# First scores of the first batch read from the feature rows in halves of 64, with the regrouping kept for what follows

## The chip, the cores and the metric

The kernel runs on one core of a Trainium2 chip. The metric is the device time of one execution in microseconds (us); the figure compared is the median over several runs. One execution was also recorded by the hardware profiler. The engines are named as in the profile: PE (TensorE matmul) with PEld (its weight loads), DVE (VectorE), ACT (ScalarE), POOL (GpSimd) and SP (the queue that issues the transfers).

## The reference

Four batches, 8 heads, 768 steps, 48 features a head. First a linear attention whose state decays by a complex factor at each step, then a mixture of four attention experts over its output, of which each row takes two.

```python
def _attn_ref(q, k, v, a_re, a_im):          # B, H, S, D = 4, 8, 768, 48
    mag = np.sqrt(a_re * a_re + a_im * a_im)
    scale = np.minimum(mag, 0.999) / (mag + 1e-06)
    a_re_n, a_im_n = (a_re * scale, a_im * scale)
    for t in range(S):
        new_re = ar * S_re - ai * S_im       # ar, ai: step t's factor
        new_im = ar * S_im + ai * S_re
        S_re, S_im = (new_re + k[t] v[t]^T, new_im)
        y[:, :, t] = q[t] . S_re

def _moe_ref(x, w_gate, wq, wk, wv, wo):     # 4 experts of width 64, 2 for each row
    logits = x @ w_gate                      # top 2, softmax over them -> w
    for e in range(E):
        q, k, v = x @ wq[e], x @ wk[e], x @ wv[e]
        a = softmax(causal(scale * q @ k^T))
        ye = a @ v @ wo[e]
        out += (w of e where e is among the row's two) * ye
```

## The kernel before

All work is recorded as a list of operations and then issued in one written order: ORDER is a permutation of the list, HOME moves single operations to another engine, ROOMS says which buffer each tile gets, and FILL[i] puts so many matmuls without a use (512 columns of a constant, written to the bank that operation i is about to write) ahead of operation i. Each engine takes its instructions strictly in that order. So what an engine does next is fixed, and an instruction that waits holds up all that stand behind it on its engine. SP takes the transfers in that order too.

A batch has three thirds of 256 steps (k = 0, 1, 2), each of two chunks of 128 steps (c = 0 to 5). For a third, `logs`, `atan`, `angles`, `sincos` and `products` turn the decay (`ab`) and q, k (`qk`) into features: the running decay is folded into q and k as exponentials and as a cosine and a sine part. This is elementwise work of ACT, DVE and POOL on tiles of 128 partitions by 768 (three groups j of 128 feature rows by 256 steps); for the very first third the three groups are worked one by one, on 256 elements. The features end in `qk`, with the 384 (head, feature) pairs along j and the partitions. Attention wants each head's 96 rows (48 cosine, 48 sine) on 96 partitions, so `regroup` copies `qk` to `fm` by ten transfers a third.

`head(b, c)` then does two things for a chunk. It transposes k (`pk`, through `ident`, copied to `kts`), and it computes the scores of the chunk's 128 steps against themselves: `psc`, one matmul of 96 rows for each head, masked with `keep` into `pts` by DVE. `state` adds v against `kts` (`pu`) to the running state and scales it with the decay at the chunk's end, a column of `fm` (`tst`). `tail` sums `pts` against v and q against the state (`yu`) and splits the result into the two parts `x` of the experts' input; after each second chunk two transfers move the last heads' rows of `x`. From there `proj` (`pp`), `vproj` (`pv`), `maxpass` (`pm`) and the experts' attention (`score`, `av`, `norm`, `wo`) go on. While PE works on one third, the others make the features of the next ones.

At the start, PE's order is: 141 fills; `psc` and `pk` of chunk 0; one fill; `yu` of chunk 0; 14 fills; `pu` of chunk 0; `psc` of chunk 1; 7 fills; `pk` and `yu` of chunk 1; `psc` of chunk 2 (its first half); `pu` of chunk 1; and so on until the first `pp`.

Of the kernel before, what the change touches and what calls it, by code (L numbers as in the profile page):

```python
# [42 lines left out]
HOME = {26: 'gpsimd',  # L43
 32: 'gpsimd',
 40: 'vector',
 48: 'vector',
# [4 lines left out]
 134: 'vector',
 145: 'vector',
 150: 'gpsimd',
 169: 'gpsimd',
 183: 'gpsimd',
 199: 'vector',
 208: 'vector',
 213: 'vector',
 220: 'gpsimd',
 287: 'gpsimd',  # L60
 296: 'vector',
 303: 'vector',
 340: 'gpsimd',
 353: 'vector',
 424: 'gpsimd',
 437: 'gpsimd',
 459: 'gpsimd',
 473: 'gpsimd',
 497: 'gpsimd',
 503: 'gpsimd',  # L70
 505: 'gpsimd',
 513: 'gpsimd',
 549: 'gpsimd',
 551: 'gpsimd',
 563: 'gpsimd',
 571: 'gpsimd',
# [8 lines left out]
 619: 'gpsimd',
 630: 'gpsimd',
 631: 'gpsimd',
 632: 'gpsimd',
# [29 lines left out]
 1109: 'vector',
 1116: 'gpsimd',
 1135: 'vector',  # L120
 1167: 'gpsimd',
 1174: 'vector',
 1176: 'vector',
 1183: 'gpsimd',
 1187: 'vector',
 1192: 'vector',
 1199: 'vector',
 1201: 'vector',
 1227: 'vector',
 1240: 'vector',  # L130
 1313: 'gpsimd',
 1320: 'gpsimd',
 1328: 'gpsimd',
# [4 lines left out]
 1354: 'vector',
 1367: 'gpsimd',
 1369: 'gpsimd',  # L140
 1374: 'gpsimd',
 1381: 'vector',
# [12 lines left out]
 1493: 'gpsimd',
# [3 lines left out]
 1512: 'vector',  # L159
 1515: 'gpsimd',  # L160
 1520: 'gpsimd',
# [3 lines left out]
 1555: 'vector',
 1564: 'gpsimd',
 1579: 'vector',
 1580: 'vector',
 1583: 'vector',
 1608: 'vector',  # L170
 1619: 'vector',
 1622: 'vector',
 1624: 'vector',
 1640: 'vector',
 1643: 'vector',
 1647: 'vector',
 1708: 'vector',
 1709: 'vector',
 1712: 'vector',
 1761: 'gpsimd',  # L180
 1763: 'gpsimd',
 1776: 'gpsimd',
 1835: 'gpsimd',
 1856: 'vector',
 1857: 'gpsimd'}

FILL = {202: 141, 204: 14, 206: 1, 210: 7, 357: 3, 406: 2, 1873: 4}

ROOMS = {'ab': [0, 1, 0, 1, 0, 1, 0, 1, 0, 1, 0, 1],
 'carry': [0, 3, 2, 3, 2, 1, 1, 3, 1, 2],  # L190
 'fm': [0, 1, 0, 1, 0, 1, 0, 1, 0, 1, 0, 1],
# [30 lines left out]

ORDER = [13, 35, 20, 0, 34, 14, 19, 33, 15, 6, 17, 118, 1, 2, 4, 18, 3, 5, 8, 119, 9, 12, 21, 120, 22, 67, 36, 68, 185, 52, 69, 53, 70, 154, 37, 54, 71, 7,
# [68 lines left out]


class View:
# [85 lines left out]
def mid(x):  # L380
    return x.bitcast(F32)
# [548 lines left out]
```

## Time and profile before

| | |
|---|---|
| median of 3 runs | 414.89 us (413.98 to 415.06) |
| profiled execution | 413.87 us, of which the span of the trace is 412.2 us |
| busy in the span: PE, DVE, ACT, POOL | 398.0, 346.3, 280.3, 157.5 us |
| PE's first matmul that is no fill | at 38.77 us |
| PE's fills before it | 141, from 6.04 us on |
| chunk 2's first score matmul | at 57.28 us |
| first `pp` of batch 0 | at 64.44 us |

Times within the trace count from the span's start. A busy share counts fills as work, so PE's 398.0 us hold a first stretch in which it does nothing that the result needs. What ends first in each stage, and who is waited for there, is read from the stage's own rows.

### The profile page before, as it was taken

To read this page: it belongs to the slowest core of one execution; us is meant where nothing else is said; L and a number is where in the kernel's file an instruction comes from. 1 tells how busy PE (TensorE), PEld (TensorE's weight loads), DVE (VectorE), ACT (ScalarE), POOL (GpSimd) and SP (SyncE) were. 2 spreads that over 40 slices of the span, in tenths; PEclk is the share of its full clock that TensorE was granted. 3 is DMA by queue.
4 is the path that set the end of the run, shared out by engine and by line. 5 is a ranking of instruction groups with operands and counts; after the bars stand their busy time and mean duration, and the time that the engine had idled before them with its cause. 6 is when DMAs were issued, how large, how long until landed. Compare 5 with 4: busy or idle time off the path is not lost. (4 is left out here: it accounts for less than half of the span.)

```text
span 412.2 us, 9649 instructions
## 1 busy us (share of the span) xinstructions
PE 398.0 (97%) x3792; PEld 326.9 (79%) x3792; DVE 346.3 (84%) x738; ACT 280.3 (68%) x436; POOL 157.5 (38%) x146
## 2 busy tenths in 40 slices
PE   4999799999999999999999999999999999999996
PEld 1445579998888779989887789989779789887775
DVE  5997979999999999999999898798794556978751
ACT  6979788986898898879688999733533222124572
POOL 0002233559373444563263324640166634002440
PEclk9999989999999999999999999999999999999999
DMA  7767808875946506828424703628003510111002
GB/s 266 281 158 202 231 0 214 231 218 132 342 117 190 154 37 164 233 63 269 126 71 116 212 3 116 191 76 233 9 2 76 165 27 2 38 45 54 2 13 103
DMA packets 27261, 53.40 MB, mean 130 GB/s; under 512 B 3536, under 2 KB 7376, under 8 KB 27216
## 3 DMA queue, kind: packets, MB, share of 16 engines
q1 hardware_dynamic: 27216, 52.78, 44.2%
q8 instruction: 30, 0.49, 0.5%
q14 instruction: 15, 0.12, 0.1%
HBM read 26.74 MB, written 4.72 MB: 76 GB/s over the span
## 5 line engine op out<-in xcount | busy, mean ns | idle before, releaser
L871 POOL TENSOR_TENSOR qk<-qk,ab 128x768 f32<-128x768 f32 x20 | 40.0, 2011 | 64.2 <-DVE qk L871 49.1
L871 ACT ACTIVATE pe<-pss 128x1024 f32<-128x1024 f32 (+2 forms) x48 | 43.4, 915 | 26.0 <-PE pss L871 22.4
L871 POOL TENSOR_SCALAR_AFFINE_SELECT pe<-pe 128x256 f32<-128x256 f32 x48 | 25.3, 544 | 84.8 <-ACT pe L871 54.8
L871 PE MATMUL pp<-x,whi 128*128 128x256 f32 x288 | 55.6, 287 | 0.1
L871 PE MATMUL psc<-fm 96*128 96x128 f32 x384 | 52.1, 281 | 0.2
L871 PEld LDWEIGHTS psc<-fm 96*128 96x128 f32 x384 | 46.6, 192 | 3.2 <-issue 0.9
L871 ACT ACTIVATE ab<-ab 128x768 f32<-128x768 f32 (+1 forms) x61 | 45.8, 762 | 4.3 <-DVE ab L871 3.2
L871 PEld LDWEIGHTS pp<-x,whi 128*128 128x128 f32 x288 | 45.4, 189 | 1.5 <-issue 1.5
L871 ACT ACTIVATE qk<-qk 128x768 f32<-128x768 f32 (+3 forms) x64 | 43.1, 684 | 4.0 <-DVE qk L871 3.6
L871 PE MATMUL pss<-qka 64*128 64x256 f32 (+3 forms) x480 | 45.5, 301 | 0.1
L871 PE MATMUL po<-pe,v 128*64 128x256 f32 (+3 forms) x320 | 42.8, 395 | 0.8 <-POOL pe L871 0.8
L869 ACT ACT_TABLE_LOAD x33 | 42.3, 1283 | 1.3 <-PEq L919 0.8
L871 POOL TENSOR_TENSOR pe<-pe 128x512 f32<-128x512 f32 (+2 forms) x25 | 31.7, 1267 | 28.6 <-DVE pe L871 13.3
L860 PEld LDWEIGHTS <-keep 128*128 128x128 bf16 x172 | 17.2, 102 | 29.8 <-issue 6.8
L871 PEld LDWEIGHTS pss<-qka 64*128 64x128 f32 x480 | 35.7, 185 | 6.2 <-issue 2.4
L871 PE MATMUL pp<-x,wlo 128*128 128x256 f32 x144 | 40.3, 280 | 0.0
L860 PE MATMUL psc<-keep 128*128 128x512 bf16 x141 | 32.9, 398 | 6.0 <-DVE keep L871 6.0
L871 DVE TENSOR_TENSOR pts<-psc,keep 128x512 f32<-128x512 f32 x48 | 32.3, 682 | 5.3 <-PE yu L871 2.9
L871 POOL TENSOR_TENSOR qk<-qk 128x768 f32<-128x768 f32 x16 | 25.8, 1620 | 23.6 <-ACT qk L871 23.4
L871 DVE CUSTOM_DVE_ANT_0 junk<-pm,negm 128x128 bf16<-128x128 f32 (+3 forms) x64 | 31.1, 485 | 3.3 <-PE pm L871 2.1
L871 PEld LDWEIGHTS po<-pe,v 128*64 128x64 f32 x320 | 20.7, 136 | 14.9 <-issue 5.0
L871 PE MATMUL pv<-whi,x 128*128 128x260 f32 x144 | 31.1, 292 | 0.0
(121 smaller groups left out, 930.6 us busy)
## 6 DMA issues: line engine op xcount, KB each, us to landing
fm<-qk SPq DMA_DIRECT2D x72, 192.8 KB, 4.7
qk<-in_ak_dram SPq DMA_DIRECT2D x12, 768.0 KB, 5.7
ab<-in_ak_dram SPq DMA_DIRECT2D x22, 384.0 KB, 4.0
vt<-in_vk_dram SPq DMA_DIRECT2D x12, 512.0 KB, 5.9
out_dram<-ob SPq DMA_DIRECT2D x24, 192.0 KB, 1.9
fm<-qk SPq DMA_DIRECT2D x24, 128.5 KB, 4.1
x<-x SPq DMA_DIRECT2D x24, 96.0 KB, 3.0
fm<-qk SPq DMA_DIRECT2D x24, 64.2 KB, 4.2
```

What stands on the lines that cost most here:

```text
L860: nc.tensor.matmul(z, real(plan.busy), real(plan.busy)[:, None, :].to_broadcast([128, 4, 128]), start=True, stop=True)
L869: nc.scalar.preload_act_table_set(need)
L871: getattr(getattr(nc, engine), name)(*a, **k)
```

## The change

For the first third of the first batch, chunks 0 and 1 no longer read `fm`. The features' rows are laid out anew by the host: each group j of 128 rows now holds one head in rows 0 to 47 and another in rows 64 to 111, and the two halves' last 16 rows hold the sixth part of heads 6 and 7. So a half of 64 rows holds a head's 48 feature rows, once in slot 0 and once in slot 1 of `qk`, and the scores of six heads are matmuls of 48 rows from `qk` itself, two that add up for each head. Heads 6 and 7 are gathered by two transfers into a new tile `hx` (`spread`). The transposes of these two chunks take all 128 rows of `qk` at once (six a chunk in place of eight). For this third `regroup` moves only what is left to read: the second chunk's q and the two decay columns. For all thirds it is eight transfers in place of ten. K and Q change places in `qk`.

```diff
-    def regroup(b, k, js=(0, 1, 2)):
+    def regroup(b, k, js):
         if (b, k) not in fm:
             fm[b, k] = p.tile([96, H, KW], F32, "fm")
-        for h, d, j, r, n in pieces():
-            if j in js:
-                p.dma(fm[b, k][2 * d:2 * d + 2 * n, h], qk[k][r:r + n, j])
+        o = C2 + C if b == k == 0 else 0
+        for j in js:
+            for i in range(2):
+                x = qk[k][64 * i + D:64 * i + 64, :, :, o:] if j == 3 else qk[k][64 * i:64 * i + D, j, :, o:]
+                p.dma(fm[b, k][:, 2 * j + i, o:], x)
+
+    hx = p.tile([128, 2, 2 * C2], F32, "hx", "pe")
+    def spread():
+        for i in range(2):
+            p.dma(hx[64 * i:64 * i + D], qk[0][64 * i + D:64 * i + 64, :, :, :2 * C2])
...
     def head(b, c):
+        k, first = c // 2, b == 0 and c < 2
+        s = slice(c % 2 * C, c % 2 * C + C)
...
+            if first:
+                pj = pk.rearrange("p (j d) -> p j d", j=3)
+                for j in range(3):
+                    p.flip((pj[:, j], qk[k][:, j, g, s], ident))
...
+        if first:
+            z = p.bank("psc", 2).rearrange("p i (j t) -> p i j t", j=4)
+            for j in range(4):
+                t = hx if j == 3 else qk[0][:, j]
+                p.mm(*((z[:, i, j], t[64 * i:64 * i + D, x, s], t[64 * i:64 * i + D, x, C2 + c * C:C2 + c * C + C], x == 0, x == 1)
+                       for x in range(2) for i in range(2)))
...
-FILL = {202: 141, 204: 14, 206: 1, 210: 7, 357: 3, 406: 2, 1873: 4}
+FILL = {201: 39, 212: 9, 214: 21, 369: 1, 381: 3, 418: 1, 1864: 3}
...
-ORDER = [13, 35, 20, 0, 34, 14, 19, 33, 15, 6, 17, 118, 1, 2, 4, 18, 3, 5, 8, 119, 9, 12, 21, 120, 22, 67, 36, 68, 185, 52, 69, 53, 70, 154, 37, 54, 71, 7,
...
```

ORDER, HOME and ROOMS are new throughout, so the order shifts on every engine. Three places matter for what follows.

On PE at the start of the program, this stood before (each score and transpose reads `fm`; the rows of the 141 fills ahead are left out):

```order
L860 LDWEIGHTS keep
L860 MATMUL psc<-keep 128x512
L871 MATMUL psc<-fm 128x128 x8
L871 MATMUL pk<-ident,fm 128x96 x8
L860 LDWEIGHTS keep
L860 MATMUL yu<-keep 128x512
L871 MATMUL yu<-pts,vt 64x128 x8
```

and this stands there now, chunks 0 and 1 together, the 39 fills (written to the bank of `pk`) and the 21 fills (bank of `yu`) shown by one row each:

```order
L903 MATMUL psc<-qk 128x128 x16
L892 LDWEIGHTS keep
L892 MATMUL pk<-keep 128x512
...
L903 MATMUL pk<-ident,qk 128x128
L903 MATMUL psc<-hx 128x128 x4
L903 MATMUL pk<-ident,qk 128x128 x10
L903 MATMUL psc<-qk 128x128 x4
L903 MATMUL psc<-hx 128x128 x4
L903 MATMUL psc<-qk 128x128 x4
L892 LDWEIGHTS keep
L892 MATMUL yu<-keep 128x512
...
L903 MATMUL yu<-pts,vt 64x128 x8
```

Half of the two chunks' scores now come ahead of the fills; the other half, and all transposes, come behind a transpose that reads `ident`.

On DVE, `ident` was made among the first instructions; before, the products of third 1 (three on DVE) were followed at once by chunk 0's masking:

```order
L871 CAST pick<-ident 32x24
L871 TENSOR_TENSOR qk<-qk,ab 128x3x256 x3
L871 TENSOR_TENSOR pts<-psc,keep 128x512 x2
L871 COPY kts<-pk 128x384
L871 SCALAR_TENSOR_TENSOR qk<-qk 128x3x256
```

Now `ident` is made behind all four products of third 1, and eleven instructions on third 2, on the second batch and on the weights (`wlo`) come ahead of the masking:

```order
L903 TENSOR_TENSOR qk<-qk,ab 128x3x256 x4
L903 TENSOR_SCALAR ident<-iota 128x128
L903 SCALAR_TENSOR_TENSOR qk<-qk 128x3x256
L903 SCALAR_TENSOR_TENSOR ab<-col,carry,ab 128x256 x3
L903 SCALAR_TENSOR_TENSOR qk<-qk 128x3x256
L903 TENSOR_TENSOR wlo<-wst,whi 128x768
L903 SCALAR_TENSOR_TENSOR qk<-cmask,qk 128x256 x3
L903 TENSOR_TENSOR ab<-ab 128x768
L903 TENSOR_TENSOR wlo<-wst,whi 128x768
L903 TENSOR_TENSOR pts<-psc,keep 128x512 x2
L903 COPY kts<-pk 128x2x3x16
```

On SP, the second batch's q and k of third 0 (the tile of `qk` that chunks 0 and 1 now read on PE) are fetched ahead of the eighth transfer of third 1, and the transfers of `x` stand behind both:

```order
L903 DMA fm<-qk 96x1x514 x7
L903 DMA qk<-in_ak_dram 128x3x512
L903 DMA fm<-qk 96x1x514
L903 DMA qk<-in_ak_dram 128x3x512
L903 DMA x<-x 16x3x512 x2
```

Before, the same fetch stood ahead of third 1's transfers too, but what read its tile was the transfers of third 0 alone.

## Rows read from the trace of the kernel before

**Rows 1.** Busy time by stage: stretch, its length, each engine's busy (instructions), PE clock, DMA.
```profile
25.54:38.84 13.30, 13.30 (x64) 6.14 (x62) 11.91 (x19) 10.98 (x15) 0.72 (x1) 1.00 0.79 201
38.84:57.27 18.43, 16.15 (x135) 11.62 (x133) 14.65 (x20) 13.41 (x17) 5.75 (x3) 0.91 0.58 167
57.27:64.44 7.17, 6.71 (x78) 5.97 (x77) 7.04 (x11) 5.02 (x8) 3.89 (x2) 1.00 0.10 27
64.44:250.00 185.56, 183.79 (x1883) 159.50 (x1882) 177.47 (x363) 161.43 (x243) 89.08 (x71) 1.00 0.56 160
```

**Rows 2.** Timeline of PE to 65 us: start, length, line, tiles, count [idle before].
```profile
6.04 32.89 PE L860 MATMUL psc<-keep 128*128 128x512 bf16 x141 [6.04 <-DVE keep L871]
38.77 1.95 PE L871 MATMUL psc<-fm 96*128 96x128 f32 x16
40.55 0.82 PE L871 MATMUL pk<-ident,fm 96*128 96x96 f32 x8
41.52 1.09 PE L871 MATMUL yu<-pts,vt 128*64 128x128 f32 x16
51.44 2.96 PE L860 MATMUL pk<-keep 128*128 128x512 bf16 x7 [1.94 <-DVE tst L871]
56.30 1.04 PE L871 MATMUL yu<-fm,tst 96*48 96x128 f32 x16
57.28 1.16 PE L871 MATMUL psc<-fm 96*128 96x128 f32 x8
58.27 1.48 PE L871 MATMUL pu<-vt,kts 128*96 128x48 f32 x16
64.44 0.36 PE L871 MATMUL pp<-x,whi 128*128 128x256 f32 x1
```

**Rows 3.** Timeline of DVE, 22 to 62 us.
```profile
22.78 2.76 DVE L871 TENSOR_TENSOR qk<-qk,ab 128x256 f32<-128x256 f32 x8
...
27.73 1.27 DVE L871 TENSOR_TENSOR_SCAN qk<-cmask,qk 128x256 f32<-128x256 uint8 x2
...
30.43 0.95 DVE L871 TENSOR_TENSOR wlo<-wst,whi 128x768 fp32r<-128x768 f32 x1
31.29 0.55 DVE L871 TENSOR_SCALAR ab<-ab 128x768 int32<-128x768 int32 x1
...
50.84 0.54 DVE L871 TENSOR_TENSOR tst<-pu,fm 96x384 f32<-96x384 f32 x1
```

**Rows 4.** Timeline of PE, 68 to 72 us: 64-row matmuls between 96-row ones.
```profile
68.77 1.05 PE L871 MATMUL psc<-fm 96*128 96x128 f32 x8
69.77 0.73 PE L871 MATMUL pm<-qka 64*128 64x128 f32 x8
```

**Rows 5.** Busy time around PE's 1.94 us of idling (columns as in rows 1).
```profile
49.50:51.44 1.94, 0.00 (x2) 0.00 (x0) 1.94 (x3) 1.04 (x2) 1.94 (x2) 1.00 0.49 124
51.44:52.40 0.96, 0.96 (x3) 0.38 (x3) 0.96 (x2) 0.96 (x2) 0.96 (x1) 0.61 0.02 6
52.40:54.20 1.80, 1.80 (x6) 0.69 (x5) 0.78 (x2) 1.77 (x3) 0.20 (x1) 0.50 0.00 0
```

**Rows 6.** Groups by shape, ACT and DVE: count, busy us, mean ns.
```profile
L869 ACT ACT_TABLE_LOAD x33 | 42.3, 1283 | 1.3 <-PEq L919 0.8
L871 ACT ACTIVATE ab<-ab 128x768 f32<-128x768 f32 x50 | 41.8, 840 | 4.2 <-DVE ab L871 3.2 <-POOL ab L871 0.7
L871 ACT ACTIVATE x<-yu 128x512 fp32r<-128x512 f32 x19 | 11.3, 594 | 21.8 <-PE yu L871 21.7
L871 DVE TENSOR_TENSOR qk<-qk,ab 128x768 f32<-128x768 f32 x24 | 22.7, 958 | 1.2 <-ACT ab L871 0.9
```

**Rows 7.** Transfers by kind, from the page: count, KB each, median us to landing.
```profile
fm<-qk SPq DMA_DIRECT2D x72, 192.8 KB, 4.7
qk<-in_ak_dram SPq DMA_DIRECT2D x12, 768.0 KB, 5.7
```

**Rows 8.** Timeline of SP, 60 to 65 us.
```profile
60.69 1.27 SPq L871 DMA_DIRECT2D x<-x  x2
```

More of the change, by code (lines that the diff above doesn't have):

```diff
@@ L55 @@
  183: 'gpsimd',
+ 184: 'gpsimd',
  199: 'vector',
[L57 to L76, printed above, removed]
+ 205: 'vector',
+ 251: 'vector',
+ 285: 'gpsimd',
+ 292: 'vector',
+ 310: 'vector',
+ 320: 'vector',
+ 352: 'gpsimd',
@@ L77 @@
+ 380: 'vector',
+ 431: 'gpsimd',
+ 436: 'gpsimd',
+ 453: 'gpsimd',
+ 463: 'gpsimd',
+ 471: 'gpsimd',
+ 498: 'gpsimd',
+ 515: 'gpsimd',
+ 517: 'gpsimd',
+ 525: 'gpsimd',
+ 536: 'vector',
+ 561: 'gpsimd',
+ 576: 'gpsimd',
+ 577: 'gpsimd',
  583: 'gpsimd',
- 585: 'gpsimd',
- 596: 'gpsimd',
+ 594: 'gpsimd',
  597: 'gpsimd',
- 598: 'gpsimd',
- 599: 'gpsimd',
- 605: 'gpsimd',
+ 609: 'gpsimd',
+ 610: 'gpsimd',
+ 611: 'gpsimd',
  617: 'gpsimd',
[L85 to L88, printed above, removed]
@@ L118 @@
[L118 to L128, printed above, removed]
- 1227: 'vector',
[L130 to L133, printed above, removed]
+ 628: 'gpsimd',
+ 636: 'gpsimd',
+ 641: 'gpsimd',
+ 643: 'gpsimd',
+ 697: 'vector',
+ 743: 'gpsimd',
+ 747: 'vector',
+ 752: 'vector',
+ 759: 'vector',
+ 762: 'vector',
+ 794: 'gpsimd',
+ 822: 'vector',
+ 873: 'gpsimd',
@@ new lines @@
+ 878: 'gpsimd',
+ 913: 'gpsimd',
+ 940: 'gpsimd',
+ 945: 'gpsimd',
+ 949: 'gpsimd',
+ 951: 'gpsimd',
+ 957: 'gpsimd',
+ 959: 'gpsimd',
+ 967: 'gpsimd',
+ 969: 'vector',
+ 975: 'vector',
+ 978: 'vector',
+ 981: 'vector',
+ 991: 'gpsimd',
+ 1003: 'gpsimd',
+ 1010: 'gpsimd',
+ 1025: 'gpsimd',
+ 1037: 'gpsimd',
+ 1039: 'gpsimd',
+ 1052: 'gpsimd',
+ 1053: 'gpsimd',
+ 1059: 'gpsimd',
+ 1070: 'gpsimd',
+ 1073: 'gpsimd',
+ 1083: 'gpsimd',
+ 1084: 'gpsimd',
+ 1085: 'gpsimd',
+ 1086: 'gpsimd',
+ 1108: 'vector',
@@ L134 @@
+ 1120: 'gpsimd',
+ 1132: 'vector',
+ 1138: 'vector',
+ 1160: 'vector',
+ 1203: 'vector',
+ 1204: 'vector',
+ 1227: 'vector',
+ 1236: 'gpsimd',
+ 1249: 'vector',
+ 1254: 'vector',
+ 1263: 'vector',
+ 1333: 'gpsimd',
  1337: 'gpsimd',
  1339: 'gpsimd',
- 1345: 'gpsimd',
  1347: 'gpsimd',
[L138 to L142, printed above, removed]
  1382: 'gpsimd',
- 1387: 'gpsimd',
- 1399: 'gpsimd',
  1409: 'gpsimd',
  1411: 'vector',
- 1420: 'vector',
+ 1414: 'vector',
@@ L158 @@
  1501: 'gpsimd',
[L159 to L161 removed]
+ 1522: 'vector',
  1525: 'gpsimd',
+ 1526: 'gpsimd',
  1527: 'gpsimd',
  1528: 'gpsimd',
[L165 to L185, printed above, removed]
[L187 to L191 removed]
+ 1550: 'vector',
+ 1562: 'gpsimd',
+ 1566: 'vector',
+ 1571: 'vector',
+ 1577: 'vector',
+ 1578: 'vector',
+ 1581: 'vector',
+ 1602: 'vector',
+ 1604: 'vector',
+ 1642: 'vector',
+ 1645: 'vector',
+ 1646: 'vector',
+ 1671: 'vector',
+ 1702: 'vector',
+ 1789: 'gpsimd',
+ 1829: 'gpsimd',
+ 1851: 'gpsimd',
+ 1862: 'vector',
+ 1865: 'vector'}
+FILL = {201: 39, 212: 9, 214: 21, 369: 1, 381: 3, 418: 1, 1864: 3}
+ROOMS = {'ab': [1, 0, 1, 0, 1, 0, 1, 0, 1, 0, 1, 0],
+ 'carry': [3, 2, 0, 1, 3, 3, 3, 1, 1, 3],
+ 'fm': [1, 0, 1, 0, 1, 0, 1, 0, 1, 0, 1, 0],
  'gcf': [0, 0, 0, 0],
@@ L467, in views @@
         t = ab[b, k][:, :, g]
-        Q, K, X, Y = (qk[k][:, g, i, o:o + C2] for i in range(2) for o in (0, C2))
+        K, Q, Y, X = (qk[k][:, g, i, o:o + C2] for i in range(2) for o in (0, C2))
         return t[:, 0], t[:, 1], Q, K, X, Y
@@ L539, in head @@
         for g in range(2):
-            if c < NC - 1:
-                pk = p.bank("pk")[:, :384].rearrange("p (i d) -> p i d", i=4)
-                p.flip(*((pk[:, i], part(b, c, 4 * g + i, 1), ident[:96, :96]) for i in range(4)))
-                p.copy(kt[b, c][:, 4 * g:4 * g + 4], pk)
-        for g in range(2):
+            pk = p.bank("pk")[:, :384]
+            if first:
+                pj = pk.rearrange("p (j d) -> p j d", j=3)
+                for j in range(3):
+                    p.flip((pj[:, j], qk[k][:, j, g, s], ident))
+                p.copy(t[:, :6].rearrange("p h (d x) -> p x h d", x=2)[:, g], pk.rearrange("p (h d) -> p h d", h=6)[:, :, :D])
+                p.copy(t[:, 6:].rearrange("p i (r j x) -> p x i j r", j=3, x=2)[:, g],
+                       pk.rearrange("p (j i d) -> p i j d", j=3, i=2)[:, :, :, D:])
+            elif c < NC - 1:
+                pi = pk.rearrange("p (i d) -> p i d", i=4)
+                p.flip(*((pi[:, i], part(b, c, 4 * g + i, 1), ident[:96, :96]) for i in range(4)))
+                p.copy(t[:, 4 * g:4 * g + 4], pi)
@@ new lines, in head @@
+        if first:
[4 more added lines that the diff above has]
+                       for x in range(2) for i in range(2)))
+        for g in range(2):
+            pt[b, c, g] = p.tile([128, 4, C], F32, "pts")
+            if first:
+                o = pt[b, c, g].rearrange("p (j i) t -> p j i t", i=2)
+                p.mul(V, o, z[:, :, 2 * g:2 * g + 2].rearrange("p i j t -> p j i t"),
+                      keep[:, None, None, :].to_broadcast([128, 2, 2, C]))
+                continue
@@ L737, in norm @@
         dn = p.bank("dn")[:, :n]
-        left = [i for u in UNITS[g] for i in u if i not in SUMS[b][pr][g]]
-        p.mm(*((dn[64 * e:64 * e + 64, cols(g, i)[0] - t0:], onecols, pe[b, pr, g, i][:, e],
-                i == 0, i == left[-1]) for i in left for e in range(2)))
+        if (b, pr, g) in SPLIT_SUMS:
+            y = pe[b, pr, g, 0]
+            hi = p.tile([128, 2, 512], F32R, "hi", "pe")[:, :, :n]
+            lo = y.bitcast(F32R)
+            p.copy(hi, y)
+            p.tt(V, lo, y, mid(hi), OP.subtract)
+            p.mm(*((dn[64 * e:64 * e + 64], oner[:, :HD], x[:, e], x is hi, x is lo) for x in (hi, lo) for e in range(2)))
+        else:
+            left = [i for u in UNITS[g] for i in u if i not in SUMS[b][pr][g]]
+            p.mm(*((dn[64 * e:64 * e + 64, cols(g, i)[0] - t0:], onecols, pe[b, pr, g, i][:, e],
+                    i == 0, i == left[-1]) for i in left for e in range(2)))
         if (b, g) not in ot:
@@ L787, in record @@
                 load_v(b, c // 2)
-                for j in range(3):
+                if b == c == 0:
+                    spread()
+                for j in range(4):
                     regroup(b, c // 2, (j,))
```

105 lines of the change are left out of this document (39 added, 66 removed), and 166 rows, old and new, of tables (ORDER, ROOMS).

## The prediction

> **What bounds the kernel now.** I read the busy time by stage first [rows 1]. From 57.27 us on, PE is the engine that is never free: 6.71 of 7.17 us, then 183.79 of 185.56. A microsecond that PE gains ahead of 57 us is therefore a microsecond of the end, unless another engine can't follow; the one that might not is DVE, busy for 177.47 of those 185.56 us. Before 57 us it is the other way round: the timeline of PE [rows 2] shows 141 fills up to 38.77, 14 fills and a wait behind the first `yu`, 1.94 us without work up to 51.44 and seven more fills. In that stretch PE waits for features that DVE and ACT make: from 25.54 to 38.84 DVE is busy for 11.91 of 13.30 us and ACT for 10.98 [rows 1]. So the question is not how early PE can begin, but when it starts chunk 2, from where on it doesn't stop: at 57.28 now, with the 1.48 us of chunk 1's `pu` still to do [rows 2]. The place to compare is thus 57.28 + 1.48 = 58.76, since the new order has that `pu` behind it when chunk 2 starts.
>
> **What the change removes.** The wait for the regrouping of the first third. Its features are complete at 22.78 + 2.76 = 25.54 [rows 3], and PE's scores begin 13.2 us later. DVE's instructions up to that point are the same but for a handful of small ones in both directions, so I keep 25.5. Half of the scores of chunks 0 and 1 can then run at 22 to 27 us.
>
> **What it puts there instead.** The other half stands behind a transpose that reads `ident`, and DVE makes `ident` only after the products of third 1. From 25.5, DVE has ten instructions on 768 elements (0.86 each when they follow each other, from 30.43 to 31.29 [rows 3]), five scans (two in 1.27 with the pipeline's overlap, 0.60 each), one scalar instruction of 0.55 and `ident` of about 0.2: 8.6 + 3.0 + 0.55 + 0.2 = 12.4, so 37.9 without a wait. In the same stretch DVE now idles 13.30 - 11.91 = 1.4 us for ACT [rows 1], which bounds it above at 39.3. I take 38.6. So PE goes on at the same moment as before (38.77); what it won is that chunk 1 comes along.
>
> From there two branches run to the masking (`pts`). *DVE's own:* three instructions of 0.86 and six scans of 0.60, 6.2 us, to 44.8; then `ab`, `wlo` and two `pts` (0.86, 0.86, 1.3), to 47.8. *By way of PE:* eleven transposes of 128 columns (eight of 96 take 0.82 [rows 2], so 0.14 each, 1.5 us) and four groups of scores, each of eight passes over half the rows. Such passes have no row with these operands. The nearest is `pm`, eight passes over 64 rows and 128 columns in 0.73, against 1.05 for eight of 96 rows [rows 4]; at most they cost the latter, and if two halves ran fully side by side 0.5. I take 0.73: 2.9 us. That ends at 43.0. ACT may only then overwrite the slot of `qk` that the scores read; its two instructions (0.84 each [rows 6]) end at 44.7, just when DVE arrives. But PE has idled by then: at 32.89 / 141 = 0.23 us each [rows 2] the 39 fills take 9.1 us and end at about 36, 2.6 us early, or less early if they too begin slowly. What that does to the clock is shown by the stall of 1.94 us: the granted clock behind it is 0.61 and then 0.50, the lower of the two levels (1.2 GHz), from 51.44 to 54.2 at least [rows 5]. In 2.8 us at that level half the work is done, so PE's part ends 1.4 us later, ACT's at 46.1, and `pts` comes at 49.1. Ends 47.8 and 49.1; I take 48.5, since the idling may be shorter than the row's or longer.
>
> The Trainium skill (TensorE: Matmul & The Clock Gate, the section on HAM oscillation) says that waits between bursts of matmuls throw the array back to the half clock and that each burst then starts cold. The trace agrees at 51.44; by the rule alone the sum would take 49.1, by the fills that run straight into the scores at 38.77 it would take 47.8.
>
> **From the masking to chunk 2.** *DVE's own:* three instructions on 768 elements, one scalar one, two copies of `kts`, a tiny one, and three on 512 elements (0.65 each): 2.6 + 0.55 + 0.7 + 0.1 + 1.95 = 5.9, then `tst` 0.54. That gives 54.9. *By PE and ACT:* `yu` 1.09, ACT's `x` 0.59, a table load 1.28, two instructions of 0.84 and a small copy of `kts` 0.25, then the last of `pu` 0.5 and `tst` 0.54: 5.9, so 54.4. DVE decides. Each hand-over between engines costs something that such a sum hasn't: from 38.84 to 57.27 DVE now idles 3.8 us [rows 1]. I add 1.0 of it (bounds 0 and 2.5). Then `yu` against the state, 1.04 [rows 2], and chunk 2 starts at 57.0. With all lower ends it is 54.5, with all upper ones 60.0.
>
> **The rest.** The gain is 58.76 - 57.0 = 1.8 us, with bounds +4.3 and -1.2. PE's other work is the same instruction for instruction; of the fills behind 57 us there are five before and after, and at the end three in place of four, worth 0.2. Two transfers a third less, and the moves of single operations between DVE, ACT and POOL, I cost at nothing: what hides them is that PE never waits for them now (its idling from 64.44 to 250 is 1.77 us in all). If DVE's cover is gone they cost what the third rival says. Sum: -2.0 us.
>
> The profiled execution took 413.87 us, so the sum makes 411.9 of it; that execution is 1.0 below the median of the runs, 414.89. The forecast is for the median: **412.9 us**, 0.5% less. About 0.3%, 1.24 us, is what a measurement of this kernel can tell from no change.
>
> **Rivals.**
> *The start gives more.* If `pts` comes at 47.8 and the hand-overs are covered, chunk 2 starts at 54.5 to 55, which is 3.8 to 4.3 us; with half of PE's 1.77 us of idling gone as well it is -4.7: 410.2. For it speaks that ACT has less to do ahead of its third table load than now; against it, that DVE is already full there.
> *The gain is hidden.* PE waits at the start for DVE as before, in other places (`ident`, then `pts`), and chunk 2 starts within 1.2 us of 58.76: 414.9. For it speaks that the masking is done only at 48.5, where chunk 0's `yu`, which needs it, begins at 41.52 now [rows 2], and that `tst` of chunk 0 comes at 55 in place of 50.84 [rows 3]; against it, that chunk 1's scores and transposes are then already done.
> *DVE can't follow behind 64 us* (the one that ends slower). By the count of instructions DVE takes four more on 768 elements of `qk` from POOL than it gives, 0.95 each [rows 6], 3.8 us, in a stretch in which it has 185.56 - 177.47 = 8.1 us free [rows 1]. Does the free time not lie where they fall, PE waits these 3.8 us there: -2.0 + 3.8, so 416.7. It decides from 3.2 us of new idling on.
> *SP's queue.* The fetch into `qk` must now wait for PE's last transpose of chunk 0, behind `yu` at about 50; the eighth transfer of third 1 stands behind it, and behind that transfer's landing a further fetch and the `x` transfers. At 50.5 + 1.0 for the issues and 4.7 to landing [rows 7] it is there at 56.2, and chunk 2's last score needs it at 59; `x` follows at about 58 and takes 3.75 to `pp` (60.69 to 64.44 [rows 2, 8]), needed at 65. So some 3 us are free; a landing that takes 8 us longer costs about 4, 416.9.
>
> **How the numbers follow.** The forecast with its own range of 410.4 to 415.9 gets 0.46 (0.34 of it below -0.3%, 0.12 within); the larger gain 0.13; the hidden one 0.17; DVE 0.18 (0.15 above +0.3%, 0.03 within); SP's queue 0.06. Faster 0.34 + 0.13 = 0.47, the same 0.12 + 0.17 + 0.03 = 0.32, slower 0.15 + 0.06 = 0.21. The range from 410.0 to 416.8 leaves out the upper part of the last two and some of the first rival, together not over 0.2.
>
> **What would show it.** Right: PE's first scores at 22 to 27 us; the first transpose at 38.1 to 39.5, with `ident` as what it waits for; the clock at 0.5 in the first microseconds behind; `pts` of chunk 0 at 47 to 50; chunk 2's first score at 55 to 59; from 65 to 250 us no more than 2 us without work on PE. Wrong if `ident` comes well before 37, if the half-row scores take over 1.05 a group, if the eighth transfer of third 1 is what chunk 2 waits for, or if PE idles by over 5 us between 65 and 250.

## The result, and the profile after

Before took 414.4 us (median of 5 runs on the same chip), the changed kernel 417.75 (416.56 to 419.42): **slower by 1.1%**, ratio 1.0108 with a 95% interval of 1.0072 to 1.0143. The forecast was 412.9 with a range up to 416.8, so it was wrong in its sign and by 4.85 us. The profiled execution took 419.34 us and spans 417.6; the one of before took 413.87 and spans 412.2. The ratios go by single runs, without those over 1.5% above the fastest of their kernel, and can differ from those of the medians (here 1.0081).

The stretch behind chunk 2's first score is the first place to look, since the forecast held it to be equal on both sides. Busy time by stage, first before, from chunk 2's first score to the end (columns as in rows 1):

```profile
57.28:412.20 354.92, 349.06 (x3519) 300.72 (x3517) 298.80 (x637) 233.69 (x359) 150.08 (x135) 1.00 0.41 117
```

The same of the changed kernel, with the stretch of [rows 1] above it, and PE's start in four steps:

```profile
42.00:44.00 2.00, 2.00 (x17) 1.67 (x17) 2.00 (x4) 1.97 (x6) 0.00 (x0) 0.63 0.83 228
44.00:46.00 2.00, 2.00 (x21) 1.78 (x19) 2.00 (x4) 1.11 (x3) 0.00 (x0) 0.50 0.85 262
46.00:48.00 2.00, 2.00 (x7) 0.73 (x6) 0.97 (x3) 1.75 (x3) 0.00 (x0) 0.50 0.99 225
48.00:50.00 2.00, 2.00 (x7) 0.75 (x6) 2.00 (x3) 1.97 (x3) 0.36 (x1) 0.66 0.99 221
...
64.44:250.00 185.56, 180.89 (x1840) 154.82 (x1836) 176.07 (x356) 158.26 (x236) 88.59 (x79) 1.00 0.58 160
60.02:417.60 357.58, 349.48 (x3502) 298.18 (x3500) 304.36 (x643) 235.18 (x359) 129.51 (x129) 1.00 0.42 117
```

Before's 354.92 us hold the `pu` of chunk 1 that the changed kernel has already done, 1.48 us [rows 2], so 353.44 stand against 357.58: the same work took **4.14 us longer**. Of these, 2.24 are idle time of PE (357.58 - 349.48 = 8.10 against 354.92 - 349.06 = 5.86) and 1.90 are busy time (349.48 against 349.06 - 1.48 = 347.58). Chunk 2 itself began at 60.02, which is 1.26 behind the break-even of 58.76. 4.14 + 1.26 = 5.4 is the difference of the two spans. This execution was one of the changed kernel's two longest runs; in three executions of kernels with the same order behind chunk 2 (below), the rest took 356.03 to 356.39, so the loss there is between 2.6 and 4.1 us.

PE's waits from 64.44 to 250 in the changed kernel (engine and tile that wait, releaser, us in total, times, longest):

```profile
PE yu L903 <- DVE pts L903: 1.4, 2, 0.9
PE psc L903 <- DVE wst L903: 0.6, 1, 0.6
PE pp L903 <- ACT pe L903: 0.6, 1, 0.6
PE pp L903 <- DVE qk L903: 0.5, 1, 0.5
PE pmr L892 <- ACT kts L903: 0.4, 1, 0.4
```

No wait stands out: nine kinds, none over 1.4 us, most of them on DVE. In the stretch PE idles 4.67 us in place of 1.77 [rows 1].

The start. Timeline of PE (columns as in rows 2):

```profile
24.99 3.78 PE L903 MATMUL psc<-qk 48*128 48x128 f32 x32 [24.99 <-DVE qk L903]
28.70 10.33 PE L892 MATMUL pk<-keep 128*128 128x512 bf16 x39
40.70 0.33 PE L903 MATMUL pk<-ident,qk 128*128 128x128 f32 x1 [1.67 <-DVE ident L903]
40.96 0.72 PE L903 MATMUL psc<-hx 48*128 48x128 f32 x8
...
43.12 1.23 PE L903 MATMUL psc<-qk 48*128 48x128 f32 x8
...
45.99 6.34 PE L892 MATMUL yu<-keep 128*128 128x512 bf16 x21
52.26 1.09 PE L903 MATMUL yu<-pts,vt 128*64 128x128 f32 x16
...
56.71 1.48 PE L903 MATMUL pu<-vt,kts 128*96 128x48 f32 x16
...
60.02 1.16 PE L903 MATMUL psc<-fm 96*128 96x128 f32 x8
```

And of DVE:

```profile
23.53 2.75 DVE L903 TENSOR_TENSOR qk<-qk,ab 128x256 f32<-128x256 f32 x8
...
34.34 0.96 DVE L903 TENSOR_TENSOR ab<-ab 128x768 f32<-128x768 f32 x1 [1.08 <-DMA ab<-in_ak_dram]
...
40.43 0.22 DVE L903 TENSOR_SCALAR ident<-iota 128x128 f32<-128x128 f32 x1
...
49.72 1.28 DVE L903 TENSOR_TENSOR pts<-psc,keep 128x512 f32<-128x512 f32 x2
...
58.23 0.55 DVE L903 TENSOR_TENSOR tst<-pu,fm 96x384 f32<-96x384 f32 x1 [1.71 <-PE pu L903]
```

The first scores began where they were forecast, at 24.99. The transposes waited for `ident`, as forecast, but until 40.65, 1.35 us past the forecast's upper bound of 39.3: the features were 0.8 us later, and DVE had waited 1.08 us for a fetch of `ab`. The granted clock fell to 0.5, the lower of the two levels (1.2 GHz), and stayed there from about 42.5 to 49.4 us (0.63 and 0.66 read as parts at either level). Under it a half-row group took 1.06 to 1.23 us in place of 0.72, and the 21 fills took 6.34 us (4.71 in an execution below in which the clock held), so that they ended 1.26 us after the masking was done (49.72 + 1.28 = 51.00).

### The profile page after: what moved, and what is told of

Its sections match the earlier page's. It is cut to its first block, busy times and chain, and to the rows that moved or that the text cites. A ratio compares the mean times of both kernels' runs of the same rounds, so it can differ in the third digit from the quotient of the medians.

```text
span 417.6 us, 9492 instructions
## 1 busy us (share of the span) xinstructions
PE 382.8 (92%) x3725; PEld 319.1 (76%) x3725; DVE 354.3 (85%) x740; ACT 282.6 (68%) x441; POOL 136.8 (33%) x143
## 4 chain that ended last, share of the span: by engine, by line
PE 62%; DVE 12%; ACT 9%; DMA 7%; SPq 5%; issue 2%; POOL 1%; DVEq 0%; ACTq 0%; POOLq 0%
PE pss L903 9%; PE pp L903 8%; PE psc L903 7%; PE po L903 7%; PE yu L903 6%; PE pw L903 6%; SPq L903 5%; DVE qk L903 5%; PE pu L903 5%; PE pv L903 4%; DMA fm<-qk 3%; PE pm L903 3%; ACT qk L903 3%; PE pk L903 3%; DMA ab<-in_ak_dram 2%; ACT ab L903 2%
## 5 line engine op out<-in xcount | busy, mean ns | idle before, releaser
L903 POOL TENSOR_SCALAR_AFFINE_SELECT pe<-pe 128x256 f32<-128x256 f32 x48 | 23.7, 511 | 84.9 <-ACT pe L903 65.7
L903 PE MATMUL psc<-fm 96*128 96x128 f32 x352 | 47.6, 281 | 0.6 <-DVE wst L903 0.6
L903 ACT ACTIVATE ab<-ab 128x768 f32<-128x768 f32 (+1 forms) x56 | 43.0, 777 | 6.1 <-DVE ab L903 4.1
L903 PEld LDWEIGHTS psc<-fm 96*128 96x128 f32 x352 | 42.5, 191 | 3.9 <-issue 1.6
L903 DVE TENSOR_TENSOR pe<-pe 128x512 f32<-128x512 f32 (+2 forms) x45 | 30.8, 685 | 4.5 <-PE po L903 2.0
L903 POOL TENSOR_TENSOR pe<-pe 128x512 f32<-128x512 f32 (+1 forms) x19 | 20.5, 1079 | 31.9 <-PE po L903 23.4
L903 PEld LDWEIGHTS pu<-vt,kts 128*96 128x96 f32 x320 | 29.3, 165 | 1.2 <-issue 0.9
L903 PE MATMUL pu<-vt,kts 128*96 128x48 f32 x320 | 29.8, 246 | 0.4 <-DMA vt<-in_vk_dram 0.4
```

Of the source, the lines that this page charges most:

```text
L903: getattr(getattr(nc, engine), name)(*a, **k)
```

## The experiments

Two theories stood at first. **T1**: the late `ident`, PE's gap and the fills at half the clock cost the gain of the start, and the end is late by as much. **T2**: the new sequence and the new division of work between DVE, ACT and POOL cost PE time behind 64 us. The rival to both was that the edit itself does it (transfers, layout).

### One instruction and one number of the start

```diff
 ORDER = [20, 33, 0, 7,
+6,
 34, 19, 14, 35, 15,
...
 150, 159, 25,
-6,
 160, 544, 201,
```

(6 is `ident`.)

> The changed kernel with one instruction moved: DVE makes ident (0.22 us) among its first instructions and no longer at 40.43. Theory of the late ident: the transposes follow the 39 fills at 39.0 without the 1.67 us of idling, the granted clock stays at 1.00 through the half-row scores (0.72 a group and not 1.06 to 1.23), ACT may overwrite the slot of qk at about 43.2 and not 46.22, the 21 fills take 4.9 us and not 6.34, chunk 0's yu comes at 49.8 to 50.3 (52.26 now) and chunk 2's first score at 57.5 to 58.0 (60.02 now): 415.3 to 415.8 for a median of 417.75. Rival, DVE's own work sets the start: the masking (pts) stays within 0.5 us of 49.72 and chunk 2 at 59.3 or later, 417.0 to 418.0. The loss behind 64 us (4.7 us of PE idling to 250) stays under both.

Measured: 417.98 us, ratio 1.0107 (1.0083 to 1.0131), the same as the changed kernel within the measurement. Timeline of PE:

```profile
38.51 0.27 PE L904 MATMUL pk<-ident,qk 128*128 128x128 f32 x1
...
44.24 6.37 PE L893 MATMUL yu<-keep 128*128 128x512 bf16 x21 [2.03 <-ACT kts L904]
50.54 1.13 PE L904 MATMUL yu<-pts,vt 128*64 128x128 f32 x16
...
58.33 2.05 PE L904 MATMUL psc<-fm 96*128 96x128 f32 x16
```

The transposes no longer wait, and the half-row groups run at 0.61 to 0.72. But the gap only moves: now the fills wait 2.03 us for a bank that ACT frees, and the clock falls there. Chunk 2 came 1.7 us earlier in this execution, and the median did not move. T1 misses; the rival's time came, though not its late chunk 2.

```diff
-FILL = {201: 39, 212: 9, 214: 21,
+FILL = {201: 39, 212: 9, 214: 4,
```

> The changed kernel with 4 fills in place of 21 ahead of chunk 0's yu. Theory of the overrunning fills: yu begins when pts is done, at 51.0 and not 52.26, everything behind it (x, table load, kts, pu, tst) moves up by as much, chunk 2 starts at 58.7 to 58.9 and the time is 1.2 us less, 416.5. Rival, the fills pay for themselves: PE idles some 3.8 us ahead of yu, the clock is at 0.50 for yu and pu (1.09 and 1.48 us now at 1.00, 3 us of work, up to 3 us more), chunk 2 starts at 60 or later and the time is 417.5 to 419. Second rival, DVE sets the start: no change, 417.4 to 418.1.

Measured: 420.09 us, 1.015 (1.0125 to 1.0174). Timeline of PE:

```profile
46.08 1.04 PE L893 MATMUL yu<-keep 128*128 128x512 bf16 x4
50.43 1.62 PE L904 MATMUL yu<-pts,vt 128*64 128x128 f32 x16 [3.31 <-DVE pts L904]
...
52.25 2.69 PE L904 MATMUL pu<-vt,kts 128*96 128x48 f32 x16
54.74 3.72 PE L893 MATMUL pu<-keep 128*128 128x512 bf16 x9
...
61.61 2.05 PE L904 MATMUL psc<-fm 96*128 96x128 f32 x16
```

`yu` does begin 1.8 us earlier, and then everything runs at half the clock: `pu` 2.69 us for 1.48, nine fills 3.72 for 2.11. The time lies above even the rival's 419: the fills that overran had been worth more than their overrun.

### The order of what follows

Each operation got a name from the function, its arguments and its place in it, so that the order of one kernel could be laid on the other. ROOMS, which says what buffer each tile gets, was laid out anew in all kernels from here on; in the one with three instructions handed to POOL (below) that leaves the time where it was, so new buffers alone hardly change it. First the changed kernel's start with before's rest:

```diff
-ORDER, HOME, FILL: those of the changed kernel
+ORDER: its first 260 operations, then the others as before has them
+HOME, FILL: of the others as before has them
```

> The changed kernel up to about chunk 2's start (its first 260 operations in its own order), and from there the order of before, with before's division between DVE, ACT and POOL and before's few fills; the transfers of the regrouping stay the changed kernel's 8 a third. Theory that the new order costs the steady stretch: PE's idling from 64.44 to 250 falls from 4.67 to 1.8 to 2.4 us, chunk 2 still starts at 59.5 to 60.5, the time is 2.5 to 3 us less than the changed kernel: 414.8 to 415.4. Rival, the edit itself does it (the regrouping in 8 transfers, the layout): PE's idling stays over 4 us and the time at 417.2 to 418.3.

Measured: 413.44 us against 414.08 of before, ratio 0.9998 (0.9967 to 1.0030). The whole loss is gone, with the edit in place; that is more than the theory expected. Busy time by stage:

```profile
61.63:414.40 352.77, 346.96 (x3503) 299.09 (x3501) 297.03 (x640) 232.98 (x357) 147.06 (x134) 1.00 0.42 118
64.44:250.00 185.56, 183.12 (x1887) 158.75 (x1884) 176.99 (x366) 160.48 (x241) 87.11 (x71) 1.00 0.56 157
```

From chunk 2's first score to the end it takes 352.77 us, 0.7 less than before's 353.44. In this execution the start was even later than in the changed kernel's own (61.63). The mirror image, before's start and code with the changed kernel's rest:

```diff
-ORDER, HOME, FILL: those of before
+ORDER: its first 260 operations, then the others as the changed kernel has them
+HOME, FILL: of the others as the changed kernel has them
```

> The kernel before up to about chunk 2's start (its first 260 operations in its own order), and from there the changed kernel's order and division between DVE, ACT and POOL (but for the carry copies and one copy of the gate, which stay on DVE); the code is that of before, regrouping in 12 transfers a third. Theory that the new order costs the steady stretch: PE's idling from 64.44 to 250 rises from 1.77 to 4 to 5.5 us, 416.9 to 418.0. Rival, the edit itself does it: 1.5 to 2.3 us of idling, 414.0 to 415.0.

Measured: 423.79 us, 1.0242 (1.0215 to 1.0270). Busy time by stage:

```profile
56.89:420.50 363.61, 353.12 (x3518) 301.90 (x3516) 308.33 (x647) 234.74 (x354) 132.04 (x130) 0.99 0.40 115
64.44:250.00 185.56, 179.25 (x1783) 153.46 (x1783) 174.70 (x352) 155.59 (x229) 87.58 (x78) 0.99 0.58 163
```

(The regrouping there has ten transfers a third, not the twelve of the expectation.) The new rest costs the old code more than either theory expected. That the edit does it is ruled out by the first of the pair; T2 stands. Is it the sequence or the division?

```diff
 changed kernel, from its 260th operation on
-HOME: the changed kernel's
+HOME: before's
```

> The changed kernel in its own order throughout, but from its 260th operation on each operation runs on the engine that had it before (DVE, ACT or POOL). Theory that the division does it (DVE took work from POOL): PE's idling from 64.44 to 250 falls from 4.7 to 2.5 us or less, 414.5 to 415.5. Theory that the sequence does it: idling of 4 us or more, 416.8 to 419, and more still where an engine now meets work that the sequence did not place for it.

```diff
 changed kernel's start, before's rest
-HOME of the rest: before's
+HOME of the rest: the changed kernel's
```

> The kernel of the experiment with the order of before behind chunk 2's start, but with the changed kernel's division between DVE, ACT and POOL. Theory that the division does it: 416.5 to 418 and 4 us of PE idling from 64.44 to 250. Theory that the sequence does it: 413 to 414.5 and 2.5 us or less, as with before's division (413.44).

Measured: 436.68 us (1.0569) for the new sequence with the old division, and 451.28 (1.0931) for the old sequence with the new one. Both miss every expectation by 17 us and more. A sequence and a division belong together; taken from different plans they cost PE 14.55 us of idling and 18.35, from 64.44 to 250. So the two can't be told apart by swapping them, and the loss is that of the pair. This also bears on the mirror image above: it lays a plan on code that the plan was not made for, so how much of its 9.7 us (423.79 - 414.08) is the plan's own is not shown.

### Single places in the new order

```diff
-DVE: 595 (qk<-qk), 361 (pts)
+DVE: 361 (pts), 595 (qk<-qk)
-DVE: 631, 402, 629 (qk<-qk and g), 661 (pts)
+DVE: 661 (pts), 631, 402, 629
-DVE: 570 (ab<-ab), 284 (wst)
+DVE: 284 (wst), 570 (ab<-ab)
```

> The changed kernel with three instructions of DVE moved ahead of one or two: the masking that PE waits for at 92.51 (0.93 us) and at 119.77 (0.42 us) ahead of the qk<-qk instructions that stand before them, and wst, for which PE waits at 70.32 (0.60 us), ahead of one on ab. Theory that single waits behind feature instructions cost the steady stretch: the three waits go, PE's idling from 64.44 to 250 falls by 1.5 to 2 us, 415.8 to 416.4 for 417.75. Rival, DVE has nothing to give: what is put off comes late itself, the idling turns up in other places, 417.2 to 418.2.

Measured: 419.5 us, ratio 1.0111 (1.0074 to 1.0148): no gain, and above the rival's 418.2. And the other cure for two of the three waits:

```diff
 HOME = {
+ 595: 'gpsimd', 629: 'gpsimd', 631: 'gpsimd',
```

> The changed kernel in its own order; three of the 128x768 instructions on qk that DVE took from POOL and behind which PE waits (DVE's at 89.48, 116.92 and 117.96) go back to POOL. Theory of the third rival (DVE took work that it has no room for): the waits at 92.51 and 119.77 go, 1.2 to 1.6 us less, 416.2 to 416.6. Rival, POOL makes them at 1.6 us each and two in a row, so the scalings and products behind them come 1.6 us or more later and PE waits for these: 417.5 to 420.

Measured: 417.52 us, 1.0090 (1.0063 to 1.0117), not told apart from the changed kernel. In its waits from 64.44 to 250 `yu` no longer waits for `pts`, but others have come:

```profile
PE po L907 <- ACT pe L907: 0.9, 1, 0.9
PE pm L907 <- ACT pe L907: 0.9, 1, 0.9
PE pm L907 <- DVE mpart L907: 0.6, 1, 0.6
```

PE idles 185.56 - 181.26 = 4.30 us in place of 4.67. This execution shows something else. Its start is the changed kernel's, and this time the clock held at 1.00 from 39.35 to 48. Timeline of PE:

```profile
40.44 0.33 PE L907 MATMUL pk<-ident,qk 128*128 128x128 f32 x1 [1.09 <-DVE ident L907]
...
58.17 2.05 PE L907 MATMUL psc<-fm 96*128 96x128 f32 x16
```

So one and the same order of the start put chunk 2 at 58.17, 60.02 and 61.63 in three kernels' executions.

### An earlier start

To learn what a start is worth, `ident` was put first on the old rest, too (the edit of the first experiment), and then the start was written anew.

> Order and division of before behind chunk 2's start, and ident made first. Theory that a start gained is a microsecond of the end where the rest can follow: chunk 2's first score at 58 to 58.5 (61.63 in the profiled execution without this edit), 411.0 to 412.2 against 413.44. Rival, DVE's own work sets the start and its passing on: 413.0 to 414.0, as in the changed kernel, where the same edit moved chunk 2 by 1.7 us and the time by nothing.

Measured: 413.53 us, 1.0019 (0.9988 to 1.0051); chunk 2 at 56.87 in the profiled execution, the rest 352.93 us. The median is the rival's, though chunk 2 came earlier than either expected.

```diff
-DVE: 175, 163, 28, 164, 165, 166, 549, 26, 210, 211 (pts)
+DVE: 175, 210, 211 (pts), 213, 163, 232, 233, 235, 217, 236, 164, 165, 166
-ACT: 25, 161, 162, 221, 222, 204, 226 (kts)
+ACT: 25, 199, 200, 204, 205, 161, 162, 221, 222, 226, 227 (kts)
-FILL: 212: 9, 214: 21
+FILL: 214: 3, 279: 16
...
```

(PE's and SP's instructions of the start were put in a new order, too.)

> As the one before, with the start written anew: all twelve transposes together, ACT copies the kts of chunk 0 before its own two instructions on qk, DVE masks (pts) right after its three scans, pu of both chunks before and behind chunk 0's yu, 3 fills in place of 21 and 16 in place of 9, the latter ahead of chunk 2; wlo and the scans of the next block stand behind them. Theory that DVE's sequence, and not the edit, held chunk 2 back: pts of chunk 0 at 43.5 to 44.5 (49.7 in the changed kernel), chunk 2's first score at 54 to 56, 407.5 to 410. Rival, DVE has no free time there: the scans that are put off by 4 to 5 us come late for chunk 4, PE waits as long there, and the time is 411 to 414.

Measured: 419.34 us, 1.0143 (1.0108 to 1.0177). Timeline of PE:

```profile
53.56 1.95 PE L913 MATMUL psc<-fm 96*128 96x128 f32 x16
...
60.03 0.55 PE L913 MATMUL pk<-ident,fm 96*128 96x96 f32 x4 [3.86 <-DVE pts L913]
...
72.17 0.73 PE L913 MATMUL pm<-qka 64*128 64x128 f32 x8 [2.62 <-ACT qka L913]
```

Chunk 2 begins 6.5 us earlier than in the changed kernel, 3.3 earlier than with `ident` first, and PE gives it back at once: DVE masks chunk 2 at 59.30. In this region DVE has no time to give, and more is lost than the rival expected. Next, a bank for the fills was freed (two more of chunk 0's transposes behind its `yu`), with 27 fills in place of 21; first on the old rest, then, with the three moves on DVE, in the new order.

```diff
-PE: 220, 198, 219, 197, 218; 214, 215 (yu), 196, 234
+PE: 220, 219, 218; 214, 215 (yu), 196, 197, 198 (transposes), 234
-FILL: 214: 21
+FILL: 214: 27
```

> Order and division of before behind chunk 2's start, ident first, the bank freed for the fills in the same way and 27 fills. In the profiled execution without the freed bank the fills waited 1.26 us for ACT, the clock stayed at 1.00 and chunk 2 began at 56.87 in 409.8 us of span, but the runs of that kernel lie between 411.0 and 418.9. Theory that the long runs are those in which the clock falls in PE's gap before the fills: without the gap the runs lie closer together and the median at 411 to 412. Rival, the spread has another cause: 413 to 414 and as wide.

> The changed kernel with all repairs at once: the three instructions ahead as in the kernel with the masks first, ident made first, two more transposes of chunk 0 put behind its yu so that a bank is free for the fills and they don't wait for ACT's copy, and 27 fills in place of 21. If the losses are these and they add: chunk 2 at 56.5 to 57.5, 1.5 to 2 us less idling, 412.8 to 414.5. If the start gives nothing to the end in this order, as the experiment with ident alone showed: 416 to 417.5.

Measured: 414.09 us, 0.9994 (0.9967 to 1.0021), and 418.55, 1.0104 (1.0083 to 1.0125). The first is close to the rival's (runs from 410.97 to 417.14, as wide as before), the second lies above both expectations. The first one's profiled execution, chunk 2 at 57.38 and a granted clock of 1.00 throughout the start, shows where the early start went. SP, then PE:

```profile
58.24 0.39 SPq L915 DMA_DIRECT2D qk<-in_ak_dram  x1
59.06 1.28 SPq L915 DMA_DIRECT2D x<-x  x2
```

```profile
65.88 0.55 PE L915 MATMUL pp<-x,whi 128*128 128x256 f32 x1 [3.56 <-DMA x<-x]
```

The `x` transfers that `pp` needs were issued right behind a fetch of 768 KB. So that fetch was put behind them:

```diff
-SP: 580 (fetch into qk), 242, 243 (x)
+SP: 242, 243 (x), 580 (fetch into qk)
 in the second and third also
-SP: 546 (fetch into qk), 273 (eighth transfer)
+SP: 273 (eighth transfer), 546 (fetch into qk)
```

> The kernel with the freed bank on the old rest, and one transfer of SP moved: the fetch of 768 KB into qk for the next block is issued behind the two x transfers (96 KB each) and not right ahead of them. Theory that the start's gain was lost in the x transfers, which queue behind that fetch (PE waited 3.56 us for them at 65.88 in that kernel's profiled execution, and 1.35, 1.8 us in others): no wait of pp for x above 0.5 us, pp at 62.5 to 63.5, the runs within 411 to 414 and the median 411 to 412. Rival, the spread and the median have another cause: 413.5 to 414.5 and runs up to 417.

> As the one before, and the eighth regrouping transfer of chunk 2 issued ahead of the first of these fetches and no longer behind it. Theory that each small transfer that PE waits for must not stand behind a fetch of 768 KB: as good or better by up to 1 us, 410.5 to 412, chunk 2's transposes without a wait for fm (0.5 us before). Rival: no difference to the one before within 0.5 us.

> The changed kernel's own order throughout, with ident first, the freed bank and 27 fills, and both transfers of SP moved as in the kernel before this one. Theory that the new order behind 64 us can't use an earlier start (DVE sets it): 416.5 to 418, chunk 2 at 56.5 to 58 and the idling from 64.44 to 250 at 5 us or more. Theory that only the x transfers kept the start's gain from the end: 413.5 to 415.5.

Measured: 412.58 us, 1.0015 (0.9983 to 1.0047); 414.20, 1.0023 (1.0000 to 1.0046); and in the new order 422.17, 1.0223 (1.0192 to 1.0254). The wait for `x` is 0.48 us in the first, so that part holds, but its runs still lie between 411.06 and 416.88. Moving the eighth transfer as well gained nothing, and where the clock held it cost time: of the runs with a mean granted clock of 0.999 or above, the median is 413.97 with the move and 412.06 without. The last is above both expectations. It has the earliest start of any kernel with the changed kernel's own sequence and division, and the longest rest; busy time by stage:

```profile
57.31:419.70 362.39, 352.31 (x3502) 300.75 (x3500) 305.12 (x643) 234.99 (x359) 129.16 (x129) 0.99 0.41 115
```

with this wait, in the timeline of PE, as its largest:

```profile
69.33 2.08 PE L904 MATMUL psc<-fm 96*128 96x128 f32 x8 [2.81 <-DVE wst L904]
```

DVE's own work is not what holds `wst` up. It stands right behind an instruction on `ab` for which DVE waited for ACT, and ACT had waited for a transfer; timelines of DVE and ACT:

```profile
67.85 0.96 DVE L904 SCALAR_TENSOR_TENSOR ab<-ab 128x768 f32<-128x768 f32 x1 [2.38 <-ACT carry L904]
```

```profile
66.88 0.84 ACT L904 ACTIVATE qk<-ab 128x768 f32<-128x768 f32 x1 [3.07 <-DMA fm<-qk]
```

In the kernel with all repairs the same instruction of ACT waited 3.31 us, for a fetch of `ab`. It began at 67.87 in the changed kernel, at 67.47 and 66.88 in these two, while chunk 2 began at 60.02, 57.66 and 57.31. So an early start runs into transfers here. And since the last kernel also holds the move of the eighth transfer, which cost time on the old rest, not all of its loss need be the start's.

Two more fillings of the gap ahead of chunk 0's `yu`, each with `x` ahead of the fetch on the old rest, asked why the runs there fall into two groups.

```diff
-FILL: 214: 27
+FILL: 214: 32 (in the second kernel 36)
```

> The kernel with x ahead of the fetch on the old rest (median 412.58), with 32 fills in place of 27 ahead of chunk 0's yu: at 0.23 us each they end 1.15 us later, where PE waited 0.85 us for the masking. Theory that the two groups of that kernel's runs (seven at 411.1 to 413.0 with a mean granted clock of 0.999 to 1.000, five at 414.5 to 416.9 with 0.991 to 0.998) are told apart by whether the clock falls in this gap: hardly a run below a mean clock of 0.998, median 411.5 to 412.5, which is faster than before by some 0.3 to 0.5%. Rival, the clock falls elsewhere (at ident, or at the transposes): the two groups stay, 412.5 to 414.

> The same with 36 fills: they end about 1.2 us behind the masking when the clock holds. Theory of the gap: no run with a fallen clock, each run some 0.7 to 1.2 us longer than the good runs of the kernel with 32, 412 to 413.2 and the narrowest spread. Rival: the two groups stay, 413 to 415.

Measured: 413.19 us, 1.0004 (0.9978 to 1.0030), and 413.23, 1.0002 (0.9978 to 1.0025). With 27 fills, five of twelve runs had a mean granted clock of 0.991 to 0.998 and took 414.5 to 416.9 us; with 32 and with 36, one of twelve was at 0.991 or 0.992 (416.4 and 415.8). So the clock fell in fewer runs, as the theory had it, though each kernel has one long run (415.26 and 415.14) with the clock at 0.999, too. The other runs became 1.0 to 1.1 us longer (their medians are 412.06, 413.08 and 413.17; the kernel with 27 fills ran on another chip), so no version is faster than before by more than the measurement can tell.

The kernel before has two such groups itself. Of its 97 runs beside these experiments, 25 had a mean granted clock of 0.998 or above, and their median is 411.46 us; the other 72 took 413.07 or longer. Where the clock holds, then, none of the three kernels is faster than before. The profiled execution of before (413.87) had 0.996, so the break-even of 58.76 is that of its longer runs; a run of the other group was not traced.

## Why the prediction was wrong

**The step that gave the sign** is the one in "The rest": PE's other work the same instruction for instruction, the moves between DVE, ACT and POOL at nothing, worth -0.2 us together. It measured +4.14 in the profiled execution, and 2.6 to 3.0 in three others with that order; the forecast's own sign for it, no more than 2 us without work on PE from 65 to 250, failed with 4.67. That it is the order of what follows, with its division and buffers, is shown by the kernel with the old rest: there the edit costs nothing (413.44). Put into the kernel before, the new rest costs 9.7 us, of which a part may be the mismatch. The time from chunk 2's first score to the end says the same in one number. With the old rest it is 353.44, 352.77, 352.93, 352.74, 352.69 and 353.31 us (before, the first kernel with it, `ident` first, `x` first, 32 and 36 fills), wherever chunk 2 began between 56.9 and 61.6. It is longer in two kernels: 356.42 with the wait of 3.56 us for `x`, and 363.04 where the start was rewritten, 3.86 and 2.62 of it in the two waits shown. With the new it is 357.58, 356.37 (`ident` first), 356.39 (few fills) and 356.03 (three to POOL), and 360 to 362 where chunk 2 was made to begin at 57.3 to 57.7. I had read "PE never waits for them now" as cover for any order. It was a property of the old order; DVE's 177.47 of 185.56 us [rows 1] are the warning that it would not hold by itself.

**The third rival** gave 416.7; with *SP's queue*, at 416.9, it came nearest to 417.75. Its premise holds: from chunk 2's first score to the end DVE is busy for 304.36 us in place of 298.80, 5.56 more (3.8 forecast), and POOL for 129.51 in place of 150.08. (The 176.07 us from 64.44 to 250 are fewer than before's 177.47, but that window does not hold the same work in both kernels.) That this is what costs the time is not shown, nor ruled out: three of the instructions handed back gain nothing that can be measured (417.52), but DVE is still busy for 303.27 us there, and putting the waited-for ones first gains nothing either. The waits change places instead.

**The start** was mis-sized, too: 57.0 forecast, 58.17 to 61.63 measured, so a gain of 1.8 us became between +0.6 and -2.9. Its terms: the features of the first third were complete at 26.28, not 25.5. `ident` was ready at 40.65, not 38.6, and outside the bounds that I drew from DVE's waits for ACT alone; the fetch of `ab` now stands among the regrouping's transfers on SP, and I had counted those as harmless. The half-row groups cost 0.72 at the full clock as estimated, and the fall of the clock behind the gap was foreseen, but not that the 21 fills would run through it (6.34 us in place of 4.71): `pts` was done at 51.0, `yu` began at 52.26. And `tst` came at 58.23, not 54.9: chunk 0's `pu` ran only from 56.71, behind nine fills, and ACT made the last `kts` copy for it at 56.80, behind `yu`, `x` and a table load.

**But the start did not decide.** In the new order an earlier chunk 2 leaves the median where it was (`ident` first) or worse (all repairs; `x` first). Nor did the clock decide: the changed kernel's run with a mean granted clock of 1.000 took 417.75 us, its two with 0.996 took 416.87 and 416.56. On the old rest it passes into the end of single executions (chunk 2 at 56.87, span 409.8; at 61.63, span 414.4), and the median still equals before's. *SP's queue* was the right place with another victim: not the eighth transfer but `x`, for which `pp` waited 1.35, 1.82 and 3.56 us in three kernels' executions.

**What stays open.** Of the 4.14 us, 1.90 are longer busy time of PE on the same instructions. Group by group against the kernel with the old rest it is spread thin; the largest is the 144 transposes behind chunk 2's first score, 18.4 us for 17.5. And no single place of the new order was found whose repair gives back a microsecond. The loss is shown to be that of sequence and division together, not of one wait; which of the two it is, and whether DVE's 5.56 us more are at the bottom of it, is not shown.

## What to carry to other kernels

Where an engine is full from start to end and the next one is at 95% beside it, that it "never waits" belongs to the present order: a change that comes with a new order has to be costed as a new order, by running the edit under the old one before judging either. A start that comes earlier is worth something only if the engines and transfers behind it deliver earlier, too: look for the next thing that is late (here DVE's masking, `x` behind a large fetch, and ACT behind a transfer) before counting the gain. Fills that seem to overrun can still be worth their time (with 4 in place of 21 the kernel took 420.09 us, not 417.75); a gap that is closed in one place can open ahead of the next wait.

## What the hardware showed

Idle time alone does not tell whether the clock falls. A gap of 1.67 us ahead of the transposes was followed by 0.63 and 0.50; one of 1.09 us in the same place left 1.00; and one of 2.05 us, in the kernel with 32 fills, left 1.00 as well (busy time by stage):

```profile
49.02:51.07 2.05, 0.00 (x0) 0.00 (x0) 2.05 (x4) 1.99 (x4) 0.98 (x1) 1.00 0.89 223
51.07:53.00 1.93, 1.93 (x24) 1.58 (x25) 1.93 (x5) 1.40 (x5) 0.75 (x1) 1.00 0.83 141
```

DVE can be held up by POOL. In the changed kernel DVE's line and POOL's, which begin together:

```profile
89.48 2.37 DVE L903 TENSOR_TENSOR qk<-qk 128x768 f32<-128x768 f32 x1
```

```profile
89.49 1.55 POOL L903 TENSOR_TENSOR qk<-qk 128x768 f32<-128x768 f32 x1
```

DVE's other instructions of this form take 0.94 to 1.16; here it takes about POOL's 1.55 and then 0.8 of its own, and the masking behind it is the one that PE waits 0.93 us for at 92.51. The Trainium skill (Trainium Architecture — The Big Picture, the section on what this means for kernel authors) says that DVE and GpSimd share a port pair under an exclusive lock. This row agrees with it, and so does a pair in the kernel before (POOL's at 48.52 for 1.58 us, DVE's at 48.62 for 2.30); that it is the lock and nothing else was not tried.
